# Fused attention, experts and gated layer on one core: where rounding steps, x sums and the last x preparation stand in the order of work

## The chip, the cores and the metric

The kernel runs on 1 core of a Trainium2 chip. The core has five engines, each with its own instruction queue, in order: PE (TensorE, matrix products into PSUM, with PEld for its weight loads), DVE (VectorE), ACT (ScalarE), POOL (GpSimd) and SP (SyncE), which here issues nearly all DMAs. An engine waits on semaphores that other engines or DMAs raise; whatever stands behind a waiting instruction on its engine waits too. The metric is the device time of one execution in microseconds (us); lower is better.

## The reference

Three layers follow each other. `setup_inputs` draws all tensors as float32; the launch hands some of them (the last layer's weights) over as 64-bit words, which the kernel rounds to float32 itself.

```
# 1 attention: batch 4, 8 heads, 576 tokens, 64 wide; k and v averaged over groups of 8 tokens
attn = softmax(q @ k_pooled.T / sqrt(64));  x = attn @ v_pooled     # x: 2304 x 512
# 2 experts: 4 of them, w1 512 x 1024, w2 1024 x 512
out = sum_e p[:, e] * (relu(x @ w1[e]) @ w2[e])
# 3 gated: h = ((x @ w1) * (x @ w2)) @ w3;  result = h @ w_out       # 1024 wide, back to 512
```

## The kernel before, in words

Every float32 factor is held as a high and a low part, and a product is three matmuls (`mm3`, L171: lines 172 to 174). `hi_lo` (L176) makes the parts: ACT copies to the high part (L177), then DVE or POOL subtracts to get the low part (L178).

**Order of work.** The order is written out by hand: each engine executes its instructions as the program lists them. The program lists work of other engines between the matmuls at numbered *places*.

1. *Attention and expert 0* (up to 250 us). Units of matmuls, 48 of them, two places each (L1111). Beside them, at places 54 to 89, the x sums for the next stage are prepared: `rows_of_x` (POOL, L829) adds high and low parts, `make_sums` (DVE, L835 to L838) forms four sums, `split_sums` (L843) splits them, `keep_sums` stores them. Weights of expert 1 are prepared by `weights_of` at places 76, 84 and 92 (L1022). An accumulation buffer shares its bytes with the buffer of x rows (`plain` from `WORK`).

2. *Experts 1 to 3*, each in three batches n = 0, 1, 2 of 768 tokens (`batch`, L1164). A batch has first products, four *sevens* (`seven`, L937, j = 0 to 3): a two by two block product by seven block products instead of eight. Each of the seven is 6 matmuls into a PSUM bank, and DVE combines them (L943: u, v, c1 twice, u, c0 twice; x is an ACT copy, L945). `c1` and `c0` go through a relu (L1153) and a split whose low part POOL makes (L178). The split of c0 is deferred (`pending`, `settle`) until the next seven's first product. Then come *second products*: 48 places of three matmuls, into 6 banks; the last two of eight rows are taken tile by tile, and at places 37, 39, ... 47 `give(m)` (DVE, L1225) adds a tile's bank to an accumulator tile `obs[m]` that `load_ob(m)` had loaded and stores it. Banks are taken in turn from eight (`bank_r`): of the sevens that follow, products 1 and 2 find free banks, product 3 needs the bank of give(0), product 6 that of give(3), product 8 that of give(5).

   Into the second products of batches 0 and 1 and the last three sevens of batches 1 and 2 the program puts 80 *rounding steps* (`Rounding.step`, L273) of the last layer's weights: a load, DVE L284, L285, L286, L288, L289, POOL L290, and a store that the following step issues (`flush`), for w3 after a DVE transpose (L321). There are three load and three store buffers. In a seven the step stands at `meanwhile` (L948). Batches 0 and 1 also fetch the operands of the next batch (`fetch_operand`, seven of 768 KB).

   The third batch (`last`) has no rounding steps in its second products: it prepares the four weights of the next expert with `weights_of` (DVE L757 to L760 into one buffer `s`, ACT, DVE L178, POOL L178) and splits five rows of w2 (`stream.split`, low part on POOL). Each of these refills a ring of four raw buffers with a DMA from SP that waits until the buffer has been read. `s` shares its bytes with the rounding steps' load buffers.

3. *The end batch* (expert 3, n = 2) prepares x for the gated layer: `load_x` at places 9 and 24 (L1255) into one buffer, `prepare_x` in three parts each; then `w_units` multiply w3 by w_out, with turned pieces of the result (`turn`, L1211) and gate weights (`load_gates`) between them.

4. *The gated layer* (from 912 us).

Of the kernel before, what the change touches and what calls it, by code (L numbers as in the profile page):

```python
# [17 lines left out]
def fused_kernel(  # L18
# [120 lines left out]
    PLAIN = WORK + XT + 3008  # L139
# [189 lines left out]
    with tc.manual_schedule():  # L329
# [452 lines left out]
        wop_home = [0, 2, 3, 4]  # L782
# [49 lines left out]
        def make_sums(r):  # L832

            sub = ALU.subtract
            nc.vector.tensor_tensor(r[:, 0, 0], r[:, 0, 1], r[:, 0, 0], op=sub)  # L835
            nc.vector.tensor_tensor(r[:, 0, 1], r[:, 1, 1], r[:, 0, 1], op=sub)
            nc.vector.tensor_tensor(r[:, 1, 1], r[:, 1, 1], r[:, 0, 0], op=sub)
            nc.vector.tensor_tensor(r[:, 1, 0], r[:, 1, 0], r[:, 1, 1], op=sub)  # L838

        def sums_of_x(kc):  # L840
            make_sums(sums_t[kc])

        def split_sums(kc):  # L843
            (_, th), (_, tl) = x_places[kc]
            hi_lo(th, tl, sums_t.pop(kc).rearrange("p n a s -> p (n a) s"))

        def enter_preps():
            late["small"] = Places(xr=Ring(plain, [WORK]))

        def enter_second_prep():  # L850
            areas["x1l"] = area("x1l", XT, F32, "s")
            late["small"].rings["xr"] = Ring(areas["x1l"], [0])

        def enter_last_prep():
            late["small"].rings["xr"] = Ring(plain, [WORK])

        def enter_weights():
            areas["x1h"] = area("x1h", XT, F32R, "wx")
            late["small"].rings["s"] = Ring(areas["x1l"], [0])

        def enter_experts():
            nonlocal dec
            x5[:] = [area(f"x5{t}", XT, F32, "x5" + t) for t in "hl"]
            areas["x1l"] = area("x1l", XT, F32R, "z7")
            z_t.append(Ring(areas["x1l"], [0]).tile([P, 2, BS], F32R))
            dec = Places(din=row(x5[0], 0, 2048, 3), store=row(x5[1], 0, HALF * 4, 3), turned=Ring(plain, [C0 + 2 * HALF_ROW]))
            xuv = {t: Ring(plain, [WORK + n * HALF_ROW]) for n, t in enumerate("xuv")}
            c_ring = Ring(plain, [C0]) + Ring(x5[1], [C1])
            late["small"] = Places(c=c_ring, s=Ring(x5[0], [0]), xr=Ring(plain, [WORK]), **xuv)
            late["gated"] = dict(xr=Ring(x5[0], [0]), s=Ring(x5[0], [0]), half=row(x5[0], 0, ROW, 2), c=c_ring,  # L870
                                 ob=Ring(plain, [WORK, WORK + ROW, C0]) + Ring(x5[1], [C1, 0]) + Ring(x5[0], [2 * ROW]), **xuv)

        def enter_w3():
# [3 lines left out]
                                   turned=Ring(plain, [WORK]) + row(x5[0], 0, ROW, 3) + row(x5[1], 0, ROW, 2))  # L877
# [4 lines left out]
        def ob_place(m, last, end):  # L882
# [3 lines left out]
            if last:  # L886
                return Ring(plain, [WORK + m * ROW]) if m < 4 else Ring(x5[1], [(m - 4) * ROW])
# [49 lines left out]
        def seven(j, sink, meanwhile=None, behind=lambda n: None):  # L937
# [74 lines left out]
        at_place(64, enter_second_prep)  # L1012
        at_place(74, enter_last_prep)
        for (b, kc), begin in zip(((b, kc) for b in order for kc in range(2)), (56, 62, 68, 73, 78, 88)):
            at_place(begin - 2, lambda b=b, kc=kc: rows_of_x(b, kc))
            at_place(begin, lambda kc=kc: sums_of_x(kc))
            at_place(begin + 1, lambda kc=kc: split_sums(kc))
            for m in range(2) if b != order[-1] else ():
                at_place(begin + 2 + m, lambda b=b, kc=kc, m=m: keep_sums(b, kc, [m]))
# [3 lines left out]
        also.setdefault(2 * 38, []).append(enter_weights)  # L1023
        for n, j in at_pairs.items():
            also.setdefault(2 * n, []).append(lambda j=j: weights_of(j))
# [17 lines left out]
        early = {n: [lambda j=j: load_gates(j)] for j, n in enumerate((3, 7, 12, 15))}  # L1043
# [118 lines left out]
        pieces_late = []  # L1162

        def batch(e, n, b):  # L1164
# [12 lines left out]
            for j in range(NJ):  # L1177
                some = []
                if j and n:
# [9 lines left out]
                if j == 3 and not last:  # L1189
                    for m in range(4):  # L1190
                        load_ob(m)
                if j == 2 and n == 0:
                    rounding.most = min(STEPS, e * PER_EXPERT)
                    rounding.load()
# [28 lines left out]
            def give(m):  # L1223
# [4 lines left out]
                elif not end:  # L1228
                    turn(m)
# [3 lines left out]
            if not last:  # L1233
                for i in range(4, 7):
                    act(4 * i - 14, lambda i=i: fetch_operand(orders[e][n + 1], i))
                for m in range(4, T):
                    act(6 + 2 * m, lambda m=m: load_ob(m))
# [43 lines left out]
        PER_EXPERT = 27  # L1281
# [160 lines left out]
```

## Time and profile before

| | us |
|---|---|
| median of 3 runs | 1190.92 (1189.98 to 1193.5) |
| profiled execution, its own time | 1192.41 |
| its span, first to last instruction | 1190.7 |
| PE busy | 1154.6 (97%) |
| DVE busy | 790.7 (66%) |
| ACT, POOL busy | 368.3, 427.7 |

The page gives busy times and the costliest groups of instructions; a PE that is "busy" may still be slow where the granted clock (1.00 is 2.4 GHz, 0.50 is 1.2 GHz) is low. The windows view gives busy time, granted clock and DMA share of a stretch; with the stretches cut at the borders of sevens (matmuls into `s`) and second products (matmuls into `g`), equal work can be compared. The timeline lists instructions in order, with the idle time ahead of each and what ended it.

### The profile page before, as it was taken

Reading aid. Unit: us, or ns where it says so; the run is one execution under the profiler, and the core shown is the slowest. Engines: PE = TensorE matmul, PEld = TensorE weight load, DVE = VectorE, ACT = ScalarE, POOL = GpSimd, SP = SyncE. Lnnn points to the kernel's source line nnn. Section 1 sums busy time; section 2 is a strip of 40 time slices with the busy share of each in tenths; the row PEclk is TensorE's granted clock in tenths of the full one; section 3 lists DMA queues with packets and bytes.
Section 4 is the critical chain, followed back from the end, with each engine's and each line's share of the span. In section 5 each row is a group of like instructions: output and inputs, shape, how many; then the busy total and the mean of one; then the engine's idle time right before and its main releaser. Section 6 shows DMA issues by size and latency. Waiting matters only on the chain.

```text
span 1190.7 us, 17096 instructions
## 1 busy us (share of the span) xinstructions
PE 1154.6 (97%) x5966; PEld 1036.2 (87%) x5966; DVE 790.7 (66%) x1452; ACT 368.3 (31%) x615; POOL 427.7 (36%) x399
## 2 busy tenths in 40 slices
PE   8999999989999999999999999999899999999998
PEld 6898888979999798989887989888678998999997
DVE  6866544555678786667788458887476866764554
ACT  4543432235313053503125421305334223230100
POOL 6965113244525256624335642425000211331211
PEclk8999999989999999999999999999999999999999
DMA  8864513446766826494943486773468063956341
GB/s 207 221 147 126 199 65 137 186 138 235 249 200 218 254 58 198 145 285 125 289 138 116 134 276 150 248 194 73 158 170 284 30 265 120 353 195 234 128 182 53
DMA packets 213766, 213.85 MB, mean 180 GB/s; under 512 B 88880, under 2 KB 169008, under 8 KB 213680
## 3 DMA queue, kind: packets, MB, share of 16 engines
q1 hardware_dynamic: 213392, 212.23, 56.5%
q8 instruction: 47, 0.77, 0.3%
q10 hardware_dynamic: 288, 0.52, 0.1%
q14 instruction: 39, 0.32, 0.1%
HBM read 140.87 MB, written 71.83 MB: 179 GB/s over the span
## 4 chain that ended last, share of the span: by engine, by line
PE 47%; DVE 12%; DMA 8%; issue 8%; SPq 3%; POOL 1%; ACT 1%; POOLq 0%; DVEq 0%; ACTq 0%
PE g L173 8%; PE g L172 8%; PE g L174 8%; PE s L172 8%; PE s L174 7%; PE s L173 7%; DMA xo<-keptx 2%; DVE plain L943 2%; DVE x5h L285 2%; DMA gate<-x5l 1%; DVE x5l L284 1%; DMA raw<-w 1%; DVE round L178 1%; DVE x5l L943 1%; SPq L1175 1%
## 5 line engine op out<-in xcount | busy, mean ns | idle before, releaser
L943 DVE TENSOR_TENSOR plain<-s,plain 128x384 f32<-128x384 f32 x300 | 158.0, 553 | 109.5 <-ACT plain L945 50.9
L172 PE MATMUL s<-xo,wh 128*128 128x384 f32 x624 | 209.8, 336 | 6.2 <-DVE ob L1225 3.5
L178 POOL TENSOR_TENSOR round<-x5l,round 128x768 fp32r<-128x768 f32 x60 | 112.0, 1867 | 287.2 <-ACT round L177 266.6
L172 PE MATMUL g<-w2l,round 128*128 128x512 f32 x522 | 206.3, 395 | 4.7 <-DVE plain L943 4.7
L174 PE MATMUL s<-xo,wh 128*128 128x384 f32 x624 | 208.7, 334 | 0.0
L173 PE MATMUL s<-xo,wl 128*128 128x384 f32 x624 | 208.6, 334 | 0.0
L173 PE MATMUL g<-w2h,round 128*128 128x512 f32 x522 | 204.9, 393 | 0.0
L174 PE MATMUL g<-w2h,round 128*128 128x512 f32 x522 | 204.8, 392 | 0.0
L172 PEld LDWEIGHTS s<-xo,wh 128*128 128x128 f32 x624 | 117.1, 188 | 10.2 <-DVE ob L1225 5.7
L172 PEld LDWEIGHTS g<-w2l,round 128*128 128x128 f32 x522 | 98.8, 189 | 26.8 <-DVE plain L943 7.3
L173 PEld LDWEIGHTS s<-xo,wl 128*128 128x128 f32 x624 | 117.2, 188 | 0.5
L174 PEld LDWEIGHTS s<-xo,wh 128*128 128x128 f32 x624 | 117.1, 188 | 0.0
L174 PEld LDWEIGHTS g<-w2h,round 128*128 128x128 f32 x522 | 98.6, 189 | 21.0
L173 PEld LDWEIGHTS g<-w2h,round 128*128 128x128 f32 x522 | 98.7, 189 | 18.9
L290 POOL TENSOR_TENSOR x5l<-x5l,x5h 128x256 uint32<-128x256 uint32 x80 | 59.4, 742 | 135.7 <-DVE x5h L289 120.5
L945 ACT ACTIVATE plain<-s 128x384 f32<-128x384 f32 x60 | 28.8, 480 | 230.3 <-PE s L174 151.7
L177 ACT ACTIVATE round<-x5l 128x768 fp32r<-128x768 f32 x60 | 50.8, 847 | 152.0 <-DVE x5l L1304 150.9
L178 POOL TENSOR_TENSOR round<-plain,round 128x768 fp32r<-128x768 f32 x27 | 50.5, 1869 | 128.5 <-ACT round L177 124.8
L284 DVE TENSOR_SCALAR x5l<-x5h 128x256 uint32<-128x256 uint32 x80 | 47.0, 587 | 52.3 <-DMA x5h<-in_moe_w_dram 21.3
L1153 ACT ACTIVATE plain<-plain 128x768 f32<-128x768 f32 x36 | 30.5, 848 | 150.2 <-DVE plain L943 150.2
L943 DVE TENSOR_TENSOR x5l<-s,plain 128x384 f32<-128x384 f32 x120 | 63.2, 551 | 14.9 <-PE s L174 10.8
L688 DVE SCALAR_TENSOR_TENSOR round<-g,round 128x384 fp32r<-128x384 f32 x48 | 26.4, 553 | 69.5 <-ACT round L687 69.3
(219 smaller groups left out, 2265.6 us busy)
## 6 DMA issues: line engine op xcount, KB each, us to landing
xo<-keptx SPq DMA_DIRECT2D x42, 768.0 KB
raw<-in_moe_w_dram SPq DMA_DIRECT2D x64, 256.0 KB
keptx<-xo SPq DMA_DIRECT2D x12, 768.0 KB
x5h<-in_moe_w_dram SPq DMA_DIRECT2D x128, 64.0 KB
x5h<-in_moe_w_dram SPq DMA_DIRECT2D x32, 256.0 KB
ob<-acc SPq DMA_DIRECT2D x24, 256.0 KB
kept<-xo SPq DMA_DIRECT2D x8, 768.0 KB
xo<-kept SPq DMA_DIRECT2D x8, 768.0 KB
```

Of the source, the lines that this page charges most:

```text
L172: nc.tensor.matmul(ps, lh, rl, start=first, stop=False)
L173: nc.tensor.matmul(ps, ll, rh, start=False, stop=False)
L174: nc.tensor.matmul(ps, lh, rh, start=False, stop=last)
L177: nc.scalar.activation(hi, src, AF.Copy)
L178: (lo_eng or nc.vector).tensor_tensor(lo, src, hi.bitcast(F32), op=ALU.subtract)
L284: nc.vector.tensor_scalar(au, h, 0x7FFFFFFF, None, op0=ALU.bitwise_and)
L285: nc.vector.tensor_scalar(h, h, 0x80000000, None, op0=ALU.bitwise_and)
L290: nc.gpsimd.tensor_tensor(au, au, l, op=ALU.add)
L688: nc.vector.scalar_tensor_tensor(hl, ps, 0.0, hh.bitcast(F32), op0=ALU.max, op1=ALU.subtract)
L943: nc.vector.tensor_tensor(to, one, two, op=ALU.add)
L945: nc.scalar.activation(x, product(j, A11, B11), AF.Copy)
L1153: nc.scalar.activation(r, r, AF.Relu)
```

## The change

- *x sums beside expert 0*: `make_sums` in two parts and `split_sums` in three (ACT; DVE half; DVE half), one part to a place; begins move from 56, 62, 68, 73, 78, 88 to 56, 62, 68, 74, 82, 89, the x rows alternate between `plain` and a second area; expert 1's `weights_of` moves to places 78, 86, 94, in two parts, which puts the low parts of its sums on DVE.
- *Rounding steps*: in a seven, `meanwhile` moves from behind the add to u to the very beginning. Batch 0 gets one step in its last seven; second products of batches 0 and 1 get 8 and 9 steps within places 1 to 28 (were 10 and 11 within 3 to 45); the third batch's second products of experts 1 and 2 get 4, at places 2, 8, 14, 20. `fetch_operand` and `load_ob` in second products are spread (places 6, 14, 22 and 10, 18).
- *Third batch*: `s` moves to `plain`, `weights_of` to places 5, 11, 17, 23, the w2 splits to 25, 27, 29, 31, 33; `load_ob` stands at places 14, 15, 16, 33, 34, 40. Tile 5 uses the bytes of tile 0, tiles 3 and 4 those of `s`.
- *Expert 3*: in batches 0 and 1 the turns of tiles 4 and 5 move to the next batch's beginning.
- *End batch*: `load_x` at places 4 and 5, into two areas (`enter_end`); `prepare_x` parts at places 12 to 32 (were 15 to 38); the turned pieces use these areas, and the first gates are loaded two units earlier.

```diff
-        wop_home = [0, 2, 3, 4]
+        wop_home = [0, 2, 4, 3]
...
+        def split_sums(kc, part):
+            (_, th), (_, tl) = x_places[kc]
+            r = sums_t[kc].rearrange("p n a s -> p (n a) s")
+            if part == 0:
+                nc.scalar.activation(th, r, AF.Copy)
+            else:
+                some = slice(2 * part - 2, 2 * part)
+                nc.vector.tensor_tensor(tl[:, some], r[:, some], th[:, some].bitcast(F32), op=ALU.subtract)
...
-                                   turned=Ring(plain, [WORK]) + row(x5[0], 0, ROW, 3) + row(x5[1], 0, ROW, 2))
+                                   turned=row(areas["x3h"], 0, ROW, 3) + row(areas["x3l"], 0, ROW, 3))
+
+        def enter_end():
+            areas["x3h"], areas["x3l"] = (area(f"x3{t}", XT, F32, "xr") for t in "hl")
+            late["small"].rings["xr"] = Ring(areas["x3h"], [0]) + Ring(areas["x3l"], [0])
...
             if last:
-                return Ring(plain, [WORK + m * ROW]) if m < 4 else Ring(x5[1], [(m - 4) * ROW])
+                return Ring(x5[1], [C1]) if m == 2 else Ring(plain, [WORK + (2, 3, 0, 0, 1, 2)[m] * ROW])
...
+            if meanwhile:
+                meanwhile()
             nc.scalar.activation(x, product(j, A11, B11), AF.Copy)
             settle()
             add(u, product(j, S2, T2), x)
-            if meanwhile:
-                meanwhile()
...
-        for (b, kc), begin in zip(((b, kc) for b in order for kc in range(2)), (56, 62, 68, 73, 78, 88)):
+        homes = ["plain", "plain", "x1l", "plain", "x1l", "x1l"]
+        for (b, kc), begin, base in zip(((b, kc) for b in order for kc in range(2)), (56, 62, 68, 74, 82, 89), homes):
...
-        at_pairs = {38: 0, 42: 1, 46: 2}
+        at_pairs = {39: 0, 43: 1, 47: 2}
...
-                if j and n:
+                if j == 0:
+                    some += turn_later
+                    turn_later[:] = []
+                if j if n else j == 3:
                     some.append(lambda: round_some(1))
...
             if not last:
                 for i in range(4, 7):
-                    act(4 * i - 14, lambda i=i: fetch_operand(orders[e][n + 1], i))
+                    act(8 * i - 26, lambda i=i: fetch_operand(orders[e][n + 1], i))
...
-                some = 10 + n
+                some = 8 + n
                 for i in range(some):
-                    act(3 + (6 * T - 6) * i // (some - 1), lambda: round_some(1))
+                    act(1 + 27 * i // (some - 1), lambda: round_some(1))
             elif not end:
-                rounding.flush()
-                for m in range(T):
-                    act(14 + m, lambda m=m: load_ob(m))
+                for m, at in enumerate((14, 15, 16, 33, 34, 40)):
+                    act(at, lambda m=m: load_ob(m))
                 for j in range(NJ):
-                    act(6 + 7 * j, lambda j=j: weights_of(j))
+                    act(5 + 6 * j, lambda j=j: weights_of(j))
+                for i in range(4):
+                    act(2 + 6 * i, lambda: round_some(1))
                 for i in range(AHEAD):
-                    act(29 + 2 * i + i // NJ, stream.split)
+                    act(25 + 2 * i, stream.split)
             else:
...
-                for kc, at in enumerate((9, 24)):
-                    act(at, lambda kc=kc: load_x(g_order[0], kc))
+                enter_end()
+                for kc in range(2):
+                    act(4 + kc, lambda kc=kc: load_x(g_order[0], kc))
                     for i in range(3):
-                        act(at + 6 + 4 * i, lambda kc=kc, i=i: prepare_x(kc, first_x[kc], kept_d[g_order[0]][kc], i))
+                        act(12 + 12 * kc + 4 * i, lambda kc=kc, i=i: prepare_x(kc, first_x[kc], kept_d[g_order[0]][kc], i))
```

## Rows read from the trace of the kernel before

**Rows 1.** Page, part 1: busy us, share of the span, instructions.
```profile
PE 1154.6 (97%) x5966; PEld 1036.2 (87%) x5966; DVE 790.7 (66%) x1452; ACT 368.3 (31%) x615; POOL 427.7 (36%) x399
```

**Rows 2.** Windows: stretch, length, busy us (count) by engine, clock, DMA share, GB/s.
```profile
472.25:501.40 29.15, 29.15 (x170) 29.14 (x168) 15.43 (x28) 14.58 (x21) 14.72 (x9) 1.00 0.42 139
501.40:534.08 32.68, 32.68 (x145) 27.03 (x145) 23.68 (x59) 2.19 (x3) 11.29 (x12) 1.00 0.94 291
406.35:438.15 31.80, 29.41 (x169) 29.09 (x168) 27.61 (x52) 11.46 (x16) 12.75 (x11) 1.00 0.47 142
438.15:472.25 34.10, 33.25 (x145) 26.81 (x145) 25.40 (x39) 14.32 (x25) 23.79 (x17) 1.00 0.43 136
595.93:628.00 32.07, 30.01 (x169) 29.05 (x168) 25.71 (x47) 10.81 (x16) 11.57 (x9) 1.00 0.40 124
628.00:664.64 36.64, 34.54 (x146) 28.09 (x145) 26.65 (x41) 15.18 (x26) 24.76 (x18) 0.95 0.46 139
755.61:790.63 35.02, 33.24 (x145) 26.81 (x145) 26.85 (x66) 3.80 (x5) 14.13 (x15) 1.00 0.96 298
790.63:823.89 33.26, 31.45 (x169) 28.87 (x168) 29.08 (x51) 10.84 (x16) 11.20 (x9) 1.00 0.53 111
823.89:911.75 87.86, 79.26 (x337) 63.76 (x337) 56.27 (x103) 36.62 (x66) 6.19 (x4) 0.96 0.56 159
240.00:260.00 20.00, 15.15 (x61) 13.15 (x60) 11.91 (x21) 8.92 (x16) 4.91 (x3) 0.83 0.43 152
```

**Rows 3.** Waits of PE: who waited for whom, us in total, times, longest.
```profile
PE g L172 <- DVE x5h L1225: 6.5, 1, 6.5
PE g L173 <- DVE round L178: 2.1, 3, 0.9
```

**Rows 4.** Timeline of ACT near 240 us: start, us, instruction, idle before.
```profile
231.55 0.47 ACT L687 ACTIVATE round<-g 128x384 fp32r<-128x384 f32 x1
239.00 0.63 ACT L177 ACTIVATE wh<-raw 128x512 fp32r<-128x512 f32 x1 [6.98 <-DMA raw<-in_moe_w_dram]
```

**Rows 5.** Timeline of SP near 234 us.
```profile
233.84 3.07 SPq L198 DMA_DIRECT2D raw<-in_moe_w_dram  x4
```

**Rows 6.** Page, part 5: DVE's adds in the sevens.
```profile
L943 DVE TENSOR_TENSOR plain<-s,plain 128x384 f32<-128x384 f32 x300 | 158.0, 553 | 109.5 <-ACT plain L945 50.9
```

**Rows 7.** Timeline in a seven with a rounding step (expert 2, n = 2).
```profile
610.72 1.27 DVE L284 TENSOR_SCALAR x5l<-x5h 128x256 uint32<-128x256 uint32 x1
...
611.96 1.84 POOL L178 TENSOR_TENSOR round<-x5l,round 128x768 fp32r<-128x768 f32 x1
612.03 1.92 DVE L285 TENSOR_SCALAR x5h<-x5h 128x256 uint32<-128x256 uint32 x1
```

**Rows 8.** Timeline of DVE past the second products of expert 1, n = 1.
```profile
408.49 0.40 DVE L284 TENSOR_SCALAR x5l<-x5h 128x256 uint32<-128x256 uint32 x1 [0.56 <-DMA wo<-x5l]
...
410.21 2.72 DVE L1225 SCALAR_TENSOR_TENSOR ob<-g,plain,ob 128x512 f32<-128x512 f32 x4
```

**Rows 9.** Timeline of DVE in second products of expert 2, n = 2.
```profile
646.91 0.95 DVE L757 TENSOR_TENSOR x5h<-raw 128x256 f32<-128x256 f32 x1 [1.74 <-POOL wl L178]
...
651.67 0.95 DVE L757 TENSOR_TENSOR x5h<-raw 128x256 f32<-128x256 f32 x1 [1.74 <-POOL wl L178]
```

**Rows 10.** Timeline of POOL there.
```profile
654.37 2.02 POOL L178 TENSOR_TENSOR wl<-x5h,wh 128x768 fp32r<-128x768 f32 x1 [2.04 <-ACT wh L177]
...
657.04 5.05 POOL L178 TENSOR_TENSOR w2l<-raw,w2h 128x512 fp32r<-128x512 f32 x4
```

**Rows 11.** Timeline of SP there.
```profile
649.62 12.83 SPq L196 DMA_DIRECT2D raw<-in_moe_w_dram  x8
662.50 2.11 SPq L1227 DMA_DIRECT2D acc<-plain  x4
```

**Rows 12.** Timeline of SP in the end batch.
```profile
851.14 0.90 SPq L774 DMA_DIRECT2D plain<-turned  x2
```

**Rows 13.** Timeline of ACT in the end batch.
```profile
854.44 0.53 ACT L177 ACTIVATE xo<-plain 128x384 fp32r<-128x384 f32 x1 [6.01 <-DMA plain<-turned]
```

More of the change, by code (lines that the diff above doesn't have):

```diff
@@ L137, in area @@
         return home.tile([P, size // 4], dtype, tag=tag, name=name)
-    PLAIN = WORK + XT + 3008
+    PLAIN = WORK + XT + 3072
     plain = area("plain", PLAIN, F32, "plain")
@@ L865, in enter_experts @@
             z_t.append(Ring(areas["x1l"], [0]).tile([P, 2, BS], F32R))
-            dec = Places(din=row(x5[0], 0, 2048, 3), store=row(x5[1], 0, HALF * 4, 3), turned=Ring(plain, [C0 + 2 * HALF_ROW]))
+            dec = Places(din=row(x5[0], 0, 2048, 3), store=row(x5[1], 0, HALF * 4, 3), turned=Ring(plain, [WORK + 4 * ROW]))
             xuv = {t: Ring(plain, [WORK + n * HALF_ROW]) for n, t in enumerate("xuv")}
             c_ring = Ring(plain, [C0]) + Ring(x5[1], [C1])
-            late["small"] = Places(c=c_ring, s=Ring(x5[0], [0]), xr=Ring(plain, [WORK]), **xuv)
+            late["small"] = Places(c=c_ring, s=Ring(x5[0], [0]), **xuv)
             late["gated"] = dict(xr=Ring(x5[0], [0]), s=Ring(x5[0], [0]), half=row(x5[0], 0, ROW, 2), c=c_ring,
@@ L1011, in fused_kernel @@
         at_place(2 * FIRST, enter_late)
-        at_place(64, enter_second_prep)
-        at_place(74, enter_last_prep)
-        for (b, kc), begin in zip(((b, kc) for b in order for kc in range(2)), (56, 62, 68, 73, 78, 88)):
+        homes = ["plain", "plain", "x1l", "plain", "x1l", "x1l"]
+        for (b, kc), begin, base in zip(((b, kc) for b in order for kc in range(2)), (56, 62, 68, 74, 82, 89), homes):
+            at_place(begin - 2, lambda base=base: prep_at(base))
             at_place(begin - 2, lambda b=b, kc=kc: rows_of_x(b, kc))
-            at_place(begin, lambda kc=kc: sums_of_x(kc))
-            at_place(begin + 1, lambda kc=kc: split_sums(kc))
+            for n in range(2):
+                at_place(begin + n, lambda kc=kc, n=n: sums_of_x(kc, n))
+            for n in range(3):
+                at_place(begin + 2 + n, lambda kc=kc, n=n: split_sums(kc, n))
             for m in range(2) if b != order[-1] else ():
-                at_place(begin + 2 + m, lambda b=b, kc=kc, m=m: keep_sums(b, kc, [m]))
+                at_place(begin + 3 + 2 * m, lambda b=b, kc=kc, m=m: keep_sums(b, kc, [m]))
             if b == order[-1]:
                 at_place(begin, lambda b=b, kc=kc: fetch_parts(b, kc))
-        at_pairs = {38: 0, 42: 1, 46: 2}
-        also.setdefault(2 * 38, []).append(enter_weights)
+        at_pairs = {39: 0, 43: 1, 47: 2}
+        also.setdefault(2 * 39, []).append(enter_weights)
         for n, j in at_pairs.items():
-            also.setdefault(2 * n, []).append(lambda j=j: weights_of(j))
+            for part in range(2):
+                also.setdefault(2 * n + part, []).append(lambda j=j, part=part: weights_of(j, part))
         def made(u):
@@ L1042, in fused_kernel @@
         first_x = []
-        early = {n: [lambda j=j: load_gates(j)] for j, n in enumerate((3, 7, 12, 15))}
+        early = {n: [lambda j=j: load_gates(j)] for j, n in enumerate((1, 7, 12, 15))}
         for m in range(2 * TPB):
@@ L1160, in round_some @@
                     rounding.step(STEPS)
-        pieces_late = []
+        pieces_late, turn_later = [], []
         def batch(e, n, b):
@@ L1188, in batch @@
                     keep_sums(b, j - 1)
-                if j == 3 and not last:
+                if j == (1 if n else 3) and not last:
                     for m in range(4):
                         load_ob(m)
-                if j == 2 and n == 0:
-                    rounding.most = min(STEPS, e * PER_EXPERT)
+                if j == 1 and n == 0 and e == 1:
+                    late["small"].rings["s"] = Ring(plain, [WORK])
+                    rounding.most = STEPS
+                if j == 1:
                     rounding.load()
@@ L1228, in give @@
                 elif not end:
-                    turn(m)
+                    if m < 4:
+                        turn(m)
+                    else:
+                        turn_later.append(lambda: turn(m))
                 else:
@@ L1280, in fused_kernel @@
         orders = {1: [2, 0, 1], 2: [1, 0, 2], 3: [2, 0, 1]}
-        PER_EXPERT = 27
         enter_experts()
```

31 lines of the change are left out of this document (15 added, 16 removed).

## The prediction

> **What bounds the kernel now.** I read four views in this order: the page, the windows, PE's waits, and then the timeline of single engines around each place where PE stood still.
>
> The page says that PE is busy for 97% of the span and DVE, the next, for 66% [rows 1]. So only what keeps PE from its matmuls counts, and it is at most some 36 us plus slow clock. The windows, cut at the borders of sevens and second products, show where. An undisturbed set of four sevens takes 29.15 us and an undisturbed second product 32.68 us (the first two of [rows 2]). Against these, six stretches of the expert batches are long (the third to the eighth row there): 31.80 - 29.15 = 2.65; 34.10 - 32.68 = 1.42; 32.07 - 29.15 = 2.92; 36.64 - 32.68 = 3.96; 35.02 - 32.68 = 2.34; 33.26 - 29.15 = 4.11. Together 17.4 us. Two more stretches are long: at the passage from expert 0 to expert 1, PE idles 20.00 - 15.15 = 4.85 us and the granted clock is 0.83; in the end batch with the w3 units PE idles 87.86 - 79.26 = 8.6 us at a mean clock of 0.96 (the last two of [rows 2], in reverse order). All of these lie where the change acts.
>
> **x sums and weights beside expert 0.** ACT finishes a relu copy at 232.0, then stands 6.98 us in the queue for raw weights whose load SP issued only at 233.84, a latency of 5.2 us [rows 4 to 5]. Every relu copy behind it is late, and PE runs out twice. The load is still issued by the first `weights_of` itself. That call now stands two places later, some 4 us, because two places are one unit (12 matmuls of 384 columns and 9 of 512, which is 12 x 29.15/168 + 9 x 32.68/144 = 4.1 us). SP's position is set by the x sums' store ahead of it, so the load starts as before, and ACT reaches it 4 us later: the wait falls from 7 to about 3 us. A relu copy may be late by about the unit that lies between a hidden block's making and its use, 4 us, before PE feels it. So this stall goes whole. What goes is the idle 4.85 us and, of a clock of 0.83 (17% of 20 us = 3.4 us), the part not already idle, about 3.1: **8.0 us**. The split of the sums costs nothing: the same DVE elements, in shorter pieces between the relu copies. The low parts of the sums that move from POOL (2.02 us for the larger one, [rows 10]) to DVE are hidden under a DVE that is 40% idle in that window.
>
> **Rounding steps in the sevens.** A seven has 29.15/4 = 7.29 us. DVE's seven adds take 7 x 0.553 = 3.9 us [rows 6]. A rounding step now stands behind u, where POOL makes the low parts of c1 and then of c0, 1.84 us each; L284 takes 1.27 us and L285 1.92 us, ending with POOL's instructions [rows 7], where beside an idle POOL L284 takes 0.40 and the whole step 1.7 (408.49 to 410.21, [rows 8]). If L285 is as short as L284 there, the step in the seven is 1.7 + 0.87 + 1.52 = 4.1 us, and 3.9 + 4.1 = 8.0 is over 7.29: DVE falls behind in each such seven until PE lacks a bank. At the seven's beginning the step meets only the c1 part, and its own POOL add is queued ahead of the c0 part, so that part can't run into it: I take 2.8 us, 3.9 + 2.8 = 6.7, and DVE keeps up. Bounds: 1.7 us (no collision) to 4.1 (both). What is late next is u, by about 2 us, inside a slack of six banks.
>
> **Rounding steps and loads in second products, n = 0 and 1.** In expert 1, n = 1, the last step starts 2 us into the following sevens, having waited for a store to land, and the gives stand behind it until 410.2 [rows 8]; PE needs the first bank 2.1 us in (two products of 29.15/28 = 1.04). Now steps end at place 28 (28 x 32.68/48 = 19 us) and gives begin at place 37 (25 us). The bytes are the same, later fetches relieve the start, fewer steps are packed closer; if they run 7 us late (the one at 408.49 stood at place 45, 30.6 us behind 373.7, so 4.2 late) they end at 26 and the six gives (0.7 each) at 32, before the sevens begin. So these stalls go. In expert 3 the two turns moved behind the sevens' start cost DVE 1.4 us there, hidden by the same slack. From these two parts: **17.4 us**, lower bound 7.
>
> **End batch.** The second half of x shares one buffer with the first; its load goes out at 851.14 and ACT gets it at 854.44, 3.3 us later [rows 12, 13]. DVE's gives are queued behind its split: PE idles 6.5 us [rows 3] at the end of the batch, and the clock falls. With two areas, free when the fourth seven has ended, both loads go out about 3 us into the second products, and all six parts are done before place 37. The gate load two units earlier and `turned` out of `s` also take away the first of the waits on L178 (2.1 us in three, [rows 3]). I keep the one at the third gate weight, 1.1 us. Of 8.6 idle, 7.5 goes, and 1.6 of slow clock: **9.1 us**. Bounds 6.5 to 10.2.
>
> **What it adds: the third batch's second products, experts 1 and 2.** Four rounding steps now stand between the four weight preparations. These come 4.76 us apart, and in each DVE idles 1.74 us, waiting for POOL to have read `s` [rows 9]. A step of 1.7 us would just fit into that gap, but in the gap POOL runs its 2.02 us split [rows 10], and the sevens show what a step does beside one [rows 7]. So the step runs behind it: 4.76 + 1.7 = 6.5 us apart. The Trainium skill, page SBUF — State Buffer, section "SBUF: two separate sides", says the same as a rule: DVE instructions in a two-port mode or with two SBUF inputs, and those of GpSimd, take a shared port pair whole, and the other one blocks. By that rule the step is never free here and the sum is the one below; without it this part costs nothing and the sum is 11 us less.
>
> The last split of a weight ends at 657.04 now, 29 us into the stretch that began at 628.00, and four w2 splits follow in 5.05 us, until 34.1 [rows 10]. Three steps more put that at 34.1 + 3 x 1.7 = 39.2; DVE comes to the stretch less late than before, which gives back some 2.2, the idle of PE there (36.64 - 34.54, [rows 2]): 37, bounds 34 and 39.2. SP is in order: its raw loads wait for these splits, and the stores of the gives went out at 662.50, behind them [rows 11]. That was harmless, for the loads of all `obs` were ahead. Now `load_ob(3)` and `load_ob(4)` (places 33, 34) stand behind the four raw loads, and `load_ob(5)` behind the landing of tile 0's store. With 3.3 us for a transfer [rows 12, 13]: load 3 out at 37.4, landed 40.7, give(3) done 41.5; PE needs its bank for product 6 at 32.7 + 5 x 1.04 = 37.9: 3.5 us lost. Store 0 out at 38.3, landed 41.6, load 5 landed 44.9, give(5) done 45.7; product 8, now due at 43.5, loses 2.2. Together 5.7; I take **5.5 us each, 11 for both**. Bounds 0 and 9 each (39.2, and a slow clock after the wait).
>
> **Sum.** 1192.4 (own time) - 8.0 - 17.4 - 9.1 + 11.0 = 1168.9. The median of the runs lies 1.5 below the profiled execution's time, so 1167.
>
> **Rivals.**
> 1. *The third batch's cost doesn't come*: the steps slip between POOL's instructions, or the loads come in time. For it: DVE idles 1.74 us per weight. Against it: [rows 7]. Time 1167 - 11 = 1156.
> 2. *It is dearer*: splits until 39.2 and a slow clock after each wait, 9 each; in expert 2 a stretch with 2.1 us of idle has a clock of 0.95 (the sixth of [rows 2]). Time 1167 + 7 = 1174, and to 1179 if half of the sevens' gain is missing too.
> 3. *The steps at the sevens' beginnings collide as before*: the collision is with whatever POOL runs, and c1's split ends about when the step starts. Then 17.4 shrinks to about 7 (the gives' part stays). Against it: POOL's order. Time 1167 + 10 = 1177, to 1185 with rival 2.
> 4. *Slower*: SP's order in the third batch. Each raw load that waits holds up rounding stores and inputs, the steps wait for these, the weights for the steps: a ring in which each of four rounds costs a transfer (3.3) more. It decides from 17 us per boundary, that is, if the fourth w2 split ends later than about 49 us into the stretch; four rounds of 3.3 on top of 39.2 give 52.4, and some 1196. Against it: three input buffers, so an input is asked for two steps ahead.
>
> **How the numbers follow.** Forecast 0.46 (1161 to 1172); rival 1 0.24; rival 2 0.14; rival 3 0.09; rival 4 0.07. The range takes rivals 1 and 2 and the cheaper end of 3: 1156 to 1179. About 0.3% (3.6 us) is what a measurement can tell from no change. Faster: the forecast, rivals 1 and 2 and nearly all of 3, 0.91; within 0.3%: the rest of 3 and a part of 4, 0.03; slower 0.06.
>
> **What would show it.** Right: sevens of 29.2 us in all batches; L284 and L285 together under 2.5 us in the sevens; no idle ACT over 4 us near 240; no wait on L1225 near the end batch's end; and, at the beginning of experts 2 and 3, PE waiting on L1225 behind SP loads that follow `raw` loads. Wrong: second products of n = 1 with gives later than the sevens' start; the end batch still waiting for `turned`; or third batches with no wait at all (rival 1).

## The result and the profile after

| | before | after | aligned (e2) | best (e9) |
|---|---|---|---|---|
| median of runs, us | 1190.45 | 1180.5 | 1171.5 | 1159.05 |
| span of the profiled execution, us | 1190.7 | 1177.7 | 1170.1 | 1157.9 |

The changed kernel takes 0.9912 times as long as the kernel before, 95% interval [0.9888, 0.9936]. It is faster, as forecast, but 13.5 us slower than the 1167 of the prediction and 1.5 us above its range. The last two columns are experiments, told below.

The page of the changed kernel, part 1, answers to [rows 1]: PE is busy for 98% of the span and idle for 22.1 us, 14 less than before. So the miss of 13 us has to be sought in PE's busy time too.

```profile
PE 1155.6 (98%) x5966; PEld 1033.6 (88%) x5966; DVE 800.6 (68%) x1464; ACT 369.6 (31%) x615; POOL 421.0 (36%) x393
```

The windows of the changed kernel, in the columns of [rows 2]. In their order: the six stretches that were long (sevens and second products of expert 1, last batch; the same of expert 2; second products of expert 3, second batch; its last sevens), the end batch, the passage near 240, an undisturbed second product, and the sevens behind the two third batches.

```profile
402.60:431.73 29.13, 29.13 (x170) 29.13 (x168) 23.82 (x44) 12.66 (x17) 13.22 (x9) 1.00 0.36 106
431.73:465.32 33.59, 33.59 (x145) 27.07 (x145) 29.07 (x49) 12.74 (x23) 21.91 (x17) 1.00 0.44 133
596.04:625.17 29.13, 29.13 (x169) 29.12 (x168) 23.70 (x44) 12.97 (x18) 13.24 (x9) 1.00 0.39 116
625.17:658.77 33.60, 33.60 (x146) 27.08 (x145) 29.20 (x50) 12.46 (x23) 21.81 (x17) 1.00 0.45 134
755.43:789.02 33.59, 33.59 (x145) 27.07 (x145) 25.02 (x59) 2.20 (x3) 10.55 (x11) 1.00 0.91 253
789.02:818.15 29.13, 29.13 (x169) 29.13 (x168) 25.06 (x47) 12.97 (x18) 13.21 (x9) 1.00 0.46 100
818.15:895.89 77.74, 77.47 (x337) 63.02 (x337) 53.31 (x98) 34.78 (x64) 3.70 (x2) 1.00 0.64 179
240.00:260.00 20.00, 20.00 (x102) 18.00 (x101) 14.89 (x24) 11.21 (x19) 5.64 (x4) 1.00 0.62 205
562.45:596.04 33.59, 33.59 (x145) 27.07 (x145) 22.61 (x55) 2.21 (x3) 10.58 (x11) 1.00 0.90 261
465.32:499.72 34.40, 31.50 (x169) 30.60 (x168) 19.43 (x35) 13.95 (x20) 17.73 (x13) 0.95 0.35 106
658.77:692.70 33.93, 29.68 (x169) 29.05 (x168) 17.83 (x32) 13.92 (x20) 17.27 (x13) 1.00 0.46 151
```

The first column is the length, the second PE's busy time. In the first nine rows the two agree within 0.3 us: the idle that the prediction counted is gone. But every second product takes 33.6 us where an undisturbed one took 32.68 [rows 2], at a full clock and with 145 matmuls as before. No wait does that: each matmul is slower. The timeline of PE inside an undisturbed second product of the changed kernel (562.45:596.04), five matmuls in a row without the third and fourth, columns start and length:

```profile
567.81 0.40 PE L174 MATMUL g<-w2h,round 128*128 128x512 f32 x1
568.04 0.39 PE L172 MATMUL g<-w2l,round 128*128 128x512 f32 x1
...
568.74 0.40 PE L172 MATMUL g<-w2l,round 128*128 128x512 f32 x1
```

From the first start to the fifth it is 0.93 us, four matmuls of 233 ns each. The first and the fifth of five in a row in the kernel before, inside 501.40:534.08:

```profile
519.80 0.39 PE L172 MATMUL g<-w2l,round 128*128 128x512 f32 x1
...
520.71 0.39 PE L173 MATMUL g<-w2h,round 128*128 128x512 f32 x1
```

Here it is 0.91 / 4 = 227 ns. The length of one instruction hides this (0.39 to 0.40 us in both, for matmuls overlap); the distance between starts shows it. The 384-column matmuls of the sevens keep their pace (29.13 against 29.15 us a set).

The two last rows of the windows are the third-batch boundaries, clean before the change (the first of [rows 2] is one of them). They are 34.40 - 29.13 = 5.3 and 33.93 - 29.13 = 4.8 us long: the cost forecast as 5.5 each. PE's waits there (the whole of them between 465 and 500 us, then between 658 and 693), who waited for whom, total, times, longest:

```profile
PE s L172 <- DVE plain L1242: 2.9, 2, 2.3
```
```profile
PE s L172 <- DVE plain L1242: 4.2, 2, 2.5
```

PE waits for the gives (L1242), and SP shows why they are late. Timeline of SP at the second boundary; L196 loads raw weights, L1187 loads an `obs`, L1244 stores one:

```profile
656.54 4.08 SPq L196 DMA_DIRECT2D raw<-in_moe_w_dram  x4
660.67 0.90 SPq L1187 DMA_DIRECT2D plain<-acc  x2
661.61 0.90 SPq L1244 DMA_DIRECT2D acc<-plain  x2
667.07 0.32 SPq L1187 DMA_DIRECT2D plain<-acc  x1
```

Four raw loads, each behind a w2 split, then load_ob(3) and (4), then the store of tile 0, and load_ob(5) only when that has landed: the order that the prediction wrote down. Load 3 goes out 660.67 - 625.17 = 35.5 us into the stretch (forecast 37.4).

### The profile page after: what moved, and what is told of

Read it like the earlier page. It is cut to its first block, busy times and chain, and to the rows that moved or that the text cites. A ratio compares the mean times of both kernels' runs of the same rounds, so it can differ in the third digit from the quotient of the medians.

```text
span 1177.7 us, 17100 instructions
## 1 busy us (share of the span) xinstructions
PE 1155.6 (98%) x5966; PEld 1033.6 (88%) x5966; DVE 800.6 (68%) x1464; ACT 369.6 (31%) x615; POOL 421.0 (36%) x393
## 4 chain that ended last, share of the span: by engine, by line
PE 76%; DVE 9%; issue 6%; DMA 4%; POOL 3%; ACT 1%; SPq 1%; POOLq 0%; DVEq 0%; ACTq 0%
PE g L173 15%; PE g L172 14%; PE g L174 14%; PE s L172 9%; PE s L174 9%; PE s L173 9%; PE x_ps L556 1%; PE sc L502 1%; DVE wl L178 1%; DVE plain L952 1%; PE at_ps L541 1%; DMA raw<-in_moe_w_dram 1%; POOL round L178 1%; POOL w2l L178 1%; DMA acc<-plain 1%
## 5 line engine op out<-in xcount | busy, mean ns | idle before, releaser
L178 POOL TENSOR_TENSOR round<-plain,round 128x768 fp32r<-128x768 f32 (+1 forms) x29 | 51.9, 1791 | 134.2 <-ACT round L177 93.7
L284 DVE TENSOR_SCALAR x5l<-x5h 128x256 uint32<-128x256 uint32 x80 | 57.4, 718 | 51.3 <-DMA gate<-x5l 28.7
L172 PE MATMUL g<-xl,round 128*128 128x384 f32 x192 | 66.4, 346 | 1.2 <-DVE round L688 1.2
```

The costliest lines, as they stand in the source:

```text
L172: nc.tensor.matmul(ps, lh, rl, start=first, stop=False)
L178: (lo_eng or nc.vector).tensor_tensor(lo, src, hi.bitcast(F32), op=ALU.subtract)
L284: nc.vector.tensor_scalar(au, h, 0x7FFFFFFF, None, op0=ALU.bitwise_and)
```

## The experiments

The full diff begins with a line that has no time of its own, and that the diff shown above leaves out: `plain` grows by 64 bytes, and every tile that is allocated behind it moves. The matmuls of a second product have z, the high and low parts of the hidden values, as their stationary operand (the one that PE holds as weights) and rows of w2 as the moving one. `round`, where z lies, began at byte 67,456 of a partition and begins at 67,520; the w2 tiles lie ahead of `plain` and stay (17,024 plus multiples of 2,048). Theory P (place) says that this slows the 512-column matmuls; its rival T that the new order of copies and transfers does. P1 is the tiles' own places, P2 the distance between the stationary z and the moving w2.

### Where the slower matmuls come from

**e1**, the kernel before with that line alone:

```diff
-    PLAIN = WORK + XT + 3008
+    PLAIN = WORK + XT + 3072
```

> The kernel before with one edit: `plain` is 64 bytes longer, as in the change, and nothing else. All tiles behind it (z and the h tiles in `round`, the x operands, the gated weights) then begin 64 bytes past a multiple of 128; the w2 tiles stay on multiples of 128. Theory P (place): a 512-column matmul takes 233 ns from start to start instead of 227, an undisturbed second product 33.4 us instead of 32.5; with some 2330 such matmuls the kernel takes 14 us more than the kernel before, about 1204. Rival T (traffic: the new order of copies and transfers beside the second products slows the matmuls): 227 ns and 1190, no change.

**e2**, the changed kernel with `plain` allocated last:

```diff
-    plain = area("plain", PLAIN, F32, "plain")
     round_ = area("round", (FC - 1) * ZT + 2 * EXTRA, F32R, "round")
     ap1 = area("ap1", 4 * XO, F32, "ap1")
+    for i in range(NB):
+        for t in "hl":
+            area(f"x{i}{t}", XT, F32, "first")
+    plain = area("plain", PLAIN, F32, "plain")
```

> The changed kernel with the areas in another order: `round`, the x operands and all x tiles ahead of `plain`, so that all of them begin on multiples of 128 bytes as before the change; `plain` keeps its new length. No instruction is added, left out or moved. Theory P: 227 ns and undisturbed second products of 32.5 us; 1180.5 - 14 = 1167 us. Rival T: 233 ns as in the changed kernel, 1180.

**e3**, all tiles moved by 64 bytes together; **e4** has the same line and `plain` 64 bytes shorter, so that only the w2 tiles and the others ahead of `round` have moved:

```diff
+        const.tile([P, 16], F32, tag="pad", name="pad")
         ident = const.tile([P, P], F32, tag="ident", name="ident")
```

> The kernel before with an unused constant of 64 bytes ahead of all pools: w2, z, x operands, gated weights, all of them 64 bytes past a multiple of 128, the distance between any two as before. Theory P1 (the tiles' own places count): second products as slow as with a longer `plain`, 1204 us or more. Theory P2 (the distance between the stationary z and the moving w2 counts, modulo 128): 227 ns, 1190. Rival T: 1190, so this kernel tells P1 from P2 only if the longer `plain` is slower.

> The kernel before with the same unused constant of 64 bytes and `plain` 64 bytes shorter: w2 64 bytes past a multiple of 128, z, x operands and gated weights on multiples. Theory P1 with z's place deciding: 227 ns, 1190 us. P1 with w2's place deciding: 233 ns, 1204. Theory P2 (distance): 233 ns, 1204. Rival T: 1190.

**e11**, `plain` 128 bytes shorter than before (3008 becomes 2880), and **e10**, a gap between the operands of the sevens:

```diff
     ap1 = area("ap1", 4 * XO, F32, "ap1")
+    area("gap", 64, F32, "gap")
```

> The kernel before with `plain` 128 bytes shorter: z and all tiles behind it move by 128 bytes against w2, so they are again multiples of 128 but 128 apart modulo 256. If the distance counts modulo 128: 227 ns and 1190 us. If it counts modulo 256 (e1 with +64 gave 233 ns, e4 with -64 gave 229): more than 227 ns, up to 239, and 1192 to 1210.

> The kernel before with an unused area of 64 bytes between the x operands of the sevens and the x tiles: z, w2 and the x operands stay on multiples of 128 bytes; the gated weights (stationary in the sevens) and expert 0's x tiles lie 64 bytes past one. If any stationary operand 64 bytes away (modulo 128) from its moving one slows a matmul, the 384-column matmuls of the sevens take some 178 ns instead of 173.6: with 168 of them in a set of four sevens and 15 such sets, 11 us more, 1202. If it is particular to z and w2 or to 512 columns: 1190, and 227 ns for the 512-column ones.

Measured: e1 1198.3 us, 1.0046 times the kernel before [1.0028, 1.0064]; e2 1171.5, 0.9822 [0.9797, 0.9846]; e3 1191.4, 1.0004 [0.9986, 1.0022]; e4 1192.7, 1.0005 [0.9989, 1.0021]; e11 1193.7, 1.0015 [1.0001, 1.0029]; e10 1193.1, 1.0015 [1.0004, 1.0027]. The same undisturbed second product (expert 2, first batch), in windows, of e1, e2, e3, e4, e11 and e10:

```profile
501.82:535.42 33.60, 33.60 (x146) 27.08 (x145) 24.01 (x60) 2.20 (x3) 11.28 (x12) 1.00 0.94 291
```
```profile
497.67:530.35 32.68, 32.68 (x145) 27.03 (x145) 19.13 (x50) 3.28 (x4) 10.66 (x11) 1.00 0.99 309
```
```profile
500.39:533.07 32.68, 32.68 (x145) 27.03 (x145) 23.38 (x59) 2.19 (x3) 11.26 (x12) 1.00 0.93 287
```
```profile
499.95:532.92 32.97, 32.97 (x146) 27.05 (x145) 23.56 (x59) 2.20 (x3) 11.25 (x12) 1.00 0.92 284
```
```profile
499.02:532.62 33.60, 33.60 (x146) 27.03 (x146) 24.34 (x60) 2.18 (x3) 11.30 (x12) 1.00 0.92 295
```
```profile
499.29:532.16 32.87, 32.87 (x146) 27.03 (x145) 23.89 (x60) 2.19 (x3) 11.29 (x12) 1.00 0.92 290
```

Theory T falls twice: e1 has the old order and the slow matmuls, e2 the new order and the fast ones. P1 falls with e3, where z and w2 both stand elsewhere and the pace is the old one. That leaves the distance between z and w2 (what else moves with z is no operand of these matmuls), but not modulo 128 as P2 had it: e11 has z moved by 128 and is as slow as e1, and e4 is not at the 233 ns that P2 gave it. Modulo 256 the rows agree: at the distance of before 32.68 (e3 too, and e2, whose distance is 9,472 bytes or 37 times 256 smaller), z 64 further 33.60 (after, e1), 128 nearer 33.60 (e11; modulo 256 that is also 128 further), 64 nearer 32.97 (e4). Other distances modulo 256 were not tried, and why the two directions differ stays open.

In e10 z and w2 are where they were, but for z's last tile, which lies in an x tile and moved: one in eight, and the stretch is 0.19 longer. Its sevens have the gated weights 64 bytes off. One set of the gated part, e10:

```profile
1095.13:1124.38 29.25, 29.25 (x170) 29.24 (x169) 18.46 (x32) 4.17 (x7) 5.60 (x3) 1.00 0.34 128
```

That is 0.1 us on 29.15, where 11 us in all were asked for by a general rule; the sets of experts 2 and 3 without a wait, whose weights moved likewise, take 29.12. The large effect belongs to the second products.

My price for it was wrong: e1 was expected at 1204 and has 1198. The 14 us took all 512-column matmuls to be hit and waits to stay as they are. But the stretches that show the slow pace add up to 10.7 us (below), and where PE waits for DVE, DVE catches up while PE is slow. The long sevens of 406.35:438.15 [rows 2], 31.80 us before, are in e1 and in e11:

```profile
407.21:437.72 30.51, 29.41 (x169) 29.08 (x168) 26.36 (x49) 11.45 (x16) 12.46 (x10) 1.00 0.45 134
```
```profile
406.32:435.45 29.13, 29.13 (x170) 29.12 (x168) 25.42 (x44) 11.46 (x16) 12.14 (x9) 1.00 0.44 132
```

e11 has the pace of e1 in every second product and yet only 1193.7 us against 1198.3: its waits give back most of the price. Why e1 gives back less stays open, and its 1.29 us alone prove nothing: in e3, at the pace of before, the same set took 33.04 us, so that executions differ by more than 1 us there. On the changed kernel the pace costs more: e2 gains 9.0 us on it. It does not gain all of the 10.7, as its third-batch boundaries (next) and one set of the gated part are longer.

### The third-batch boundary

In e2 the two boundaries take:

```profile
461.98:497.67 35.69, 31.48 (x169) 30.61 (x168) 18.19 (x34) 13.93 (x20) 18.09 (x13) 0.95 0.33 103
654.01:689.31 35.30, 31.25 (x169) 30.64 (x168) 19.44 (x34) 14.06 (x21) 19.00 (x13) 0.95 0.46 151
```

Over 29.15 that is 6.5 and 6.2. Of the 12.7, 8.3 are PE's four waits for the gives (now L1245); in the rest the clock is at 0.95. **e5**, on e2:

```diff
                 for i in range(AHEAD):
-                    act(25 + 2 * i, stream.split)
+                    act(41 + i, stream.split)
```

> The aligned kernel (e2) with the five w2 splits of the third batch's second products of experts 1 and 2 moved from places 25, 27, 29, 31, 33 to places 41 to 45, behind the issue of load_ob(3), (4) and (5); the four rounding steps stay. Theory S (the boundary costs time because on SP the obs loads stand behind raw loads that wait for these splits): PE's two waits at each of the two boundaries and the slow clock behind them go; 2 x (4.5 + 1.7) = 12.4 us of e2's 1171.5, so about 1160 (1158 to 1164). Rival D (the four rounding steps make DVE and POOL late; the gives come late whatever SP does): no more than a third of it, 1168 to 1172.

**e6**, on e2:

```diff
-                some = 8 + n
+                some = 10 + n
...
-                for i in range(4):
-                    act(2 + 6 * i, lambda: round_some(1))
```

> The aligned kernel (e2) with the four rounding steps taken out of the third batch's second products (experts 1 and 2) and two more in each second product of the first two batches, as many in all as there are to do; the splits stay at places 25 to 33. Theory of the prediction (three or four steps of 1.7 us each put the last w2 split, and with it the obs loads, 5 to 7 us later): the waits at the two boundaries go, about 1160 us, up to 1164 if ten or eleven steps make the gives of the first two batches late again. Rival (SP's order alone costs it, with or without steps, as load 5 waits for a store's landing anyway): half or more stays, 1166 to 1171.

Measured: e5 1162.9 us, 0.9757 [0.9736, 0.9777]; e6 1164.0, 0.9767 [0.974, 0.9794]. The boundaries of e5, then of e6 with, behind them, the sevens that follow its first two batches of expert 2:

```profile
461.67:493.26 31.59, 29.72 (x170) 29.07 (x168) 17.16 (x33) 13.96 (x20) 17.72 (x13) 1.00 0.32 96
649.59:680.88 31.29, 29.75 (x170) 29.10 (x168) 17.51 (x32) 13.94 (x20) 18.16 (x13) 1.00 0.46 152
```
```profile
461.56:490.70 29.14, 29.14 (x169) 29.14 (x168) 19.46 (x35) 13.34 (x19) 15.20 (x10) 1.00 0.24 71
650.17:679.32 29.15, 29.15 (x170) 29.14 (x168) 19.05 (x34) 13.42 (x20) 15.39 (x10) 1.00 0.41 139
523.38:554.55 31.17, 29.70 (x169) 29.05 (x168) 27.49 (x57) 11.45 (x16) 14.56 (x11) 1.00 0.68 215
587.23:617.49 30.26, 29.45 (x169) 29.12 (x168) 26.53 (x53) 11.45 (x16) 13.42 (x10) 1.00 0.49 143
```

Both edits work, so neither the steps nor SP's order is the cause alone: the loads are late because steps delay the splits *and* the loads stand behind them. Rival D and the rival of e6 fall. Each edit leaves something: e5 2.4 and 2.1 us (PE now waits for DVE's adds and ACT's copies of x in the sevens), e6 2.0 and 1.1 where its two further steps went, the old stall of the first batches: PE waits for late gives there (1.5 and 0.8 us). **e9** takes e5 and half of e6: e5 with two steps (`range(2)`) in the third batch and `some = 9 + n`.

> e5 (aligned, w2 splits at places 41 to 45) with two rounding steps instead of four in the third batch's second products, at places 2 and 8, and one more in each second product of the first two batches (9 and 10). If steps and SP's order add up as e5 and e6 show them (e5 keeps 4.1 us of waits at the two boundaries, e6, with two more steps in the first two batches, has none there and 2.6 us at other boundaries): about 1159 (1157 to 1162). If the waits that e5 keeps do not depend on the number of steps: 1163.

Measured: 1159.05 us, 0.9729 [0.9708, 0.975], below both kernels. Its boundaries:

```profile
462.14:491.28 29.14, 29.14 (x169) 29.14 (x168) 17.91 (x33) 13.97 (x20) 16.50 (x11) 1.00 0.28 87
647.62:676.76 29.14, 29.14 (x169) 29.14 (x168) 17.19 (x32) 14.01 (x21) 16.68 (x11) 1.00 0.44 147
```

### The gains, one by one, taken back from e2

**e7** puts the seven's rounding step behind u again:

```diff
-            if meanwhile:
-                meanwhile()
             nc.scalar.activation(x, product(j, A11, B11), AF.Copy)
             settle()
             add(u, product(j, S2, T2), x)
+            if meanwhile:
+                meanwhile()
```

> The aligned kernel (e2) with the rounding step (and the late turns) of a seven put back behind the sum u, where it stood before the change. Theory of the prediction (behind u a step meets POOL's two low parts, L284 and L285 take 3.2 us and DVE falls behind): the sevens of the second and third batches of experts 1 to 3 become long again, by 2 to 4 us a set as before the change; five such sets, 10 us: 1181 (1177 to 1184). Rival (the long sevens of before came from the late gives of the second products ahead of them, and the step's place is worth little): 1171 to 1174.

Measured: 1183.65 us, 12.2 more than e2; the rival's price falls. But the time is not where I expected it. In e7: last sevens of expert 1, a second product of expert 2, a boundary, last sevens of expert 3, end batch:

```profile
399.77:428.91 29.14, 29.14 (x169) 29.14 (x168) 23.51 (x39) 11.46 (x16) 12.15 (x8) 1.00 0.44 141
562.54:596.51 33.97, 33.24 (x145) 26.81 (x145) 24.76 (x62) 3.28 (x4) 12.74 (x13) 1.00 0.89 258
658.91:697.19 38.28, 32.29 (x169) 31.48 (x168) 17.99 (x32) 15.23 (x22) 22.22 (x17) 0.91 0.46 145
791.70:822.58 30.88, 29.71 (x169) 29.03 (x168) 24.77 (x43) 10.50 (x15) 9.75 (x7) 1.00 0.44 86
822.58:902.03 79.45, 77.04 (x337) 62.77 (x337) 60.97 (x108) 36.72 (x67) 7.22 (x5) 1.00 0.65 184
```

The first set, long before the change, stays clean, and so does the same set of expert 2. So the step's place is not what made these two long, and the rival's reason, late gives ahead of them, fits e6, where late gives bring long sevens back. With the step behind u the stretches behind a set pay: 1.3 us in the second row, 3.0 more than e2 at the boundary (2.9 at the other one), 2.8 more than e2's end batch (76.68, below); only the last sevens are longer themselves, by 1.7. As the boundaries were clean before the change, what the place was worth in the kernel before is not shown. At the head of the second products PE waits for the last adds of the set (L955; 0.7 us in the second row, 2.2 in the last): DVE leaves the set late.

**e8** puts the end batch's x into one buffer again:

```diff
-            late["small"].rings["xr"] = Ring(areas["x3h"], [0]) + Ring(areas["x3l"], [0])
+            late["small"].rings["xr"] = Ring(areas["x3h"], [0])
...
-                for kc in range(2):
-                    act(4 + kc, lambda kc=kc: load_x(g_order[0], kc))
+                for kc, at in enumerate((9, 24)):
+                    act(at, lambda kc=kc: load_x(g_order[0], kc))
                     for i in range(3):
-                        act(12 + 12 * kc + 4 * i, ...
+                        act(at + 6 + 4 * i, ...
```

> The aligned kernel (e2) with the end batch's two halves of x in one buffer again, loaded at places 9 and 24 and prepared from places 15 and 30, as before the change; the other parts of the change stay. Theory of the prediction (the second half's late load holds DVE's split and the gives behind it): a stretch of idle PE of about 6.5 us and slow clock come back ahead of the gated part: 1178 (1176 to 1182). Rival (the earlier gate loads and the turned tiles' own areas are what took the end batch's wait away): 1171 to 1174.

Measured: 1176.7 us, 5.2 more than e2. The end batch of e2, then of e8 with PE's first wait in it:

```profile
812.97:889.65 76.68, 76.50 (x338) 62.99 (x338) 53.53 (x98) 34.65 (x64) 3.72 (x2) 1.00 0.64 182
```
```profile
812.88:895.14 82.26, 78.34 (x338) 64.03 (x338) 52.82 (x98) 34.76 (x64) 3.71 (x2) 0.98 0.59 169
```
```profile
PE g L175 <- DVE x5h L1245: 3.7, 1, 3.7
```

The wait on the gives returns, 3.7 us instead of the 6.5 of [rows 3], and the clock falls again. The rival falls. Whether the earlier gate loads and the areas of the turned tiles took the rest, no run shows.

**e12** puts the first three weight preparations two places earlier again:

```diff
-        at_pairs = {39: 0, 43: 1, 47: 2}
-        also.setdefault(2 * 39, []).append(enter_weights)
+        at_pairs = {38: 0, 42: 1, 46: 2}
+        also.setdefault(2 * 38, []).append(enter_weights)
```

> The aligned kernel (e2) with the first three gated weight preparations at units 38, 42, 46 as before the change instead of 39, 43, 47; the sums in small steps stay. Theory of the prediction (a call two places later meets its raw loads 4 us riper; that is what removed the passage's wait): ACT waits some 4 us longer in its queue near 240 and part of the 8.0 us comes back, 1173 to 1179. Rival (the sums in small steps and the later stores took the wait away, the call's place does not matter): 1170 to 1172.

Measured: 1171.5 us, no change from e2. The passage from 225 us to the first sevens, in the kernel before, the changed one, e2 and e12 (from the same time, not from the same matmul: compare the counts):

```profile
225.12:282.69 57.57, 52.72 (x246) 46.73 (x246) 30.66 (x44) 22.36 (x38) 24.58 (x17) 0.94 0.46 151
```
```profile
225.05:277.14 52.09, 50.84 (x252) 45.19 (x251) 36.59 (x53) 21.50 (x36) 16.67 (x10) 1.00 0.54 172
```
```profile
225.11:276.38 51.27, 50.05 (x248) 44.69 (x248) 35.91 (x52) 21.36 (x36) 16.59 (x10) 1.00 0.53 175
```
```profile
225.09:276.45 51.36, 49.60 (x246) 44.15 (x245) 33.61 (x53) 22.36 (x38) 16.96 (x11) 1.00 0.58 186
```

The theory of the prediction falls: with the sums in small steps the call's place does not matter. Without them it was not tried. The timelines of e12 show another way to the same end: SP issues the raw loads at 224.73, behind two stores of x sums, where the kernel before and e2 issue them behind four, at 233.84 and 233.51; and ACT copies them at 232.46 without a wait. Of what else the change does there (the sums in small steps, their later stores, their buffers, the two-part preparation) the runs single out nothing.

## Why the prediction was wrong

The direction was right and every wait was named, but the time lies outside the range, through one step that isn't there. The first part of the prediction takes 32.68 us as the price of an undisturbed second product and measures all excess from it; the second part prices the instructions that the diff adds and moves. The diff's first line adds none, so it was passed over, and no rival lets PE itself slow down. So the step that failed is the 32.68 us, taken over for the changed kernel without a reason: e1 and e2 show that this line alone makes the price 33.60.

Step by step, from the spans (before 1190.7, forecast 1190.7 - 23.5 = 1167.2, after 1177.7, e2 1170.1). They miss by 10.5 us, the medians by 13.5, mainly as the profiled execution was 1.5 us above the median before and 0.7 below it after:

| term, us | forecast | after | e2 |
|---|---|---|---|
| passage from expert 0 to 1 | -8.0 | -5.5 | -6.3 |
| six long stretches | -17.4 | -14.7 | -17.4 |
| end batch | -9.1 | -10.1 | -11.2 |
| two third-batch boundaries | +11.0 | +10.0 | +12.7 |
| second sevens of the gated part | 0 | +0.7 | +1.5 |
| other second products (five in experts, six gated) | 0 | +6.7 | 0 |

The column of after sums to -12.9 (measured -13.0), that of e2 to -20.7 (-20.6). The slow pace stands in three of these terms, together about 10.7 us: 0.92 for each of the eight second products of the experts (three in the six stretches, five in the last row), 2.2 in the gated part, 1.1 in the end batch (77.74 - 76.68). The 0.8 between the passages is not pace: the last 447 matmuls ahead of the first sevens take 91.39 us after (185.75:277.14) and 91.50 in e2 (184.88:276.38).

- **Passage.** Over-sized by 1.7 in e2, and its reason is not needed for the gain (e12). A wait of 2.60 us for a raw load remained in ACT at 239.30 after the change, about the 3 forecast; e12 has none there, and the same time. The size is known to some 2 us only: the last 447 matmuls take 98.16 us in the profiled execution of before (184.53:282.69), and 95.6 to 96.4 in e1, e3, e4, e10 and e11, which leave this part as it was.
- **Sevens and second products.** Right as a term: in e2 all six are clean, -17.4 to the tenth. The last of the six, 33.26 us before:

```profile
783.82:812.97 29.15, 29.15 (x170) 29.15 (x169) 26.30 (x49) 12.87 (x18) 13.50 (x9) 1.00 0.51 107
```

  The part of the gives rests on a misreading and came out by luck. The steps of before stood within places 3 to 33, not 3 to 45 as said above, so the one at 408.49 was 12.3 us late (place 33 is at 396.2), not 4.2. By that lateness the new steps would have ended some 33 us into the second products, with late gives again. They run 5.1 late: in expert 1, n = 1, of the changed kernel the last one starts at 393.67 (place 28 is at 388.6), the gives at 396.74. DVE's step in a seven of the changed kernel shows the rest of the mechanism half right. The first two instructions of a step, and POOL beside them:

```profile
541.28 1.94 DVE L284 TENSOR_SCALAR x5l<-x5h 128x256 uint32<-128x256 uint32 x1
543.26 0.30 DVE L285 TENSOR_SCALAR x5h<-x5h 128x256 uint32<-128x256 uint32 x1
```
```profile
541.23 1.85 POOL L178 TENSOR_TENSOR round<-plain,round 128x768 fp32r<-128x768 f32 x1 [9.49 <-DMA ob<-acc]
```

  L284 and L285 take 2.24 us together, under the 2.5 asked for, and only the first runs beside POOL's part of c1. The step ends at 544.42, 3.1 us instead of 2.8. The Trainium skill, page SBUF — State Buffer, section "SBUF: two separate sides", says that of two such instructions the one that starts first keeps the shared ports to its end while the other waits. The trace agrees: POOL's starts first and ends at 543.08, L284 at 543.22. What I had wrong is who pays: e7 shows that in the aligned kernel the step's place costs the stretches behind a set, and only in the last one the set itself.
- **End batch.** Right and under-sized by 1 (after) to 2 us (e2). e8 shows that the two buffers with their early loads are worth 5.6 of the 11.2.
- **Third batch.** Right in mechanism and place, and e5 and e6 show both of its links. The weight preparations come 6.5, 6.3 and 6.5 us apart (L757 at 630.60, 637.11, 643.41 and 649.94), as forecast. That the size fits (5.3 and 4.8 for 5.5 each) is in part luck: PE waits 2.9 and 4.2 us where the sum had 5.7, and the remaining 2.4 and 0.5, with a clock of 0.95 at the first boundary, stood in its upper bound only. At the old pace it is dearer, 6.5 and 6.2.
- **The rivals.** Rival 1 is refuted by the waits; rival 2 came half true in e2, but is not what made the changed kernel late; 3 and 4 did not occur. The measured 1180.5 lies where rival 3 (1177 to 1185) had put it, for another reason.

## What to carry to other kernels

Read every line of a diff that changes a size or an order of allocation as a change to all tiles behind it, and check the pace of matmuls (start to start) in an undisturbed stretch before looking for waits. When a chain of delays has two links, as steps and queue order here, cutting one and halving the other (e9) can do what cutting one cannot. A cost on an engine's own speed and its waits do not add: what one takes the other partly gives back (e11), so price them together.

## What the runs showed of the hardware that was not expected

- The pace of a 512-column fp32r matmul depends on where its stationary operand lies against its moving one in a partition: 227 ns from start to start at the distance of the kernel before, 233 with z 64 or 128 bytes off (33.60 against 32.68 us for a second product), in between with w2 64 bytes further (32.97). Moving both by 64 bytes changes nothing. The 384-column matmuls with the weights 64 bytes off lose little (29.25 against 29.15 us for a set).
- The third-batch waits cost no less in a faster kernel: at the old pace the two boundaries are 11.7 to 12.9 us longer than clean sevens (e2, e8 and e12), of which PE's waits are 7.2 to 8.5; at the slow pace 10.0, with waits of 7.1 (one execution of each kernel).
